# Attention feeding a mixing MLP on one core: the rest keys' P.V moved behind the full keys, the mixing moved half a step, a second operand preparation moved forward

## Chip, cores and metric

One core of a Trainium2 chip runs the whole computation in one program. The metric is device time in microseconds (us), the median of three runs. The engines are PE (matmuls), DVE (vector), ACT (activations), POOL (here only an issuer of DMAs) and SP (issuer of DMAs).

## The reference

Attention with 4 batches, 12 heads, 448 tokens, head size 64, then a token mixing of rank 32 and an MLP of width 3072:

```python
scores = cap * tanh((q @ k.T) / sqrt(D) / cap)
attn = exp(scores - max) / (sum + 1e-9)
x = (attn @ v)                          # heads side by side: [B, S, 768]
u = x + (x.T @ U @ V).T                 # U [448, 32], V [32, 448]
out = u + relu(u @ w_ch1) @ w_ch2       # 768 -> 3072 -> 768
```

## The kernel before

**Order of the work.** The program is written as tasks with priorities, rough durations and buffers (class `Plan`). `simulate` (line 136) plays the tasks through a small model of the five engines and so fixes one order for each engine's queue; `emit` writes the instructions in that order. On the chip every engine works its queue in order and waits at semaphores. A lower priority number goes first. A buffer of a tag is given out strictly in the order in which the tasks were created (`rooms`, line 148): where the next buffer of a tag isn't to be had, later ones of that tag wait too. `SWITCH` (line 88) is what the model charges PE for a change of the task's `mode`.

**Attention.** 24 pairs of heads, worked four pairs at a time (`four`, line 452). The 448 keys of a head are three full tiles of 128 (t = 0, 1, 2) and a rest of 64 keys; the rests of two pairs are put together into one rest tile (t = 3). `steps` lists 14 score tiles for four pairs; two steps share one `th` tile. Each step: scores on PE (L503) into one of two PSUM buffers, tanh on ACT (L510), and per `th` tile one exp in place (L521). For each half (two pairs, h = 0, 1) follow the products with V: the rest keys (`rest`, L546, for both pairs into both banks `o` and `o2`), then the full keys of each pair (`full`, L561), and a copy of each bank to `u` (L274 or L272). For the first half of all, two full tiles run even earlier (`early`, L537). DVE adds up the exp tiles over the key tiles (`es`, L567), which the row sums need.

**Normalizing** (`normalize`, line 585). For two pairs: row sums on PE (L600, with ones) into a `misc` bank, a copy to `sr`, three small DMAs by POOL with a reciprocal between the first two (L607, L616, L611, L624) that bring the reciprocals to all rows as `rb`, and a product on DVE (L629).

**Mixing** (`mixin`, line 634). For two pairs: transposes on PE (L650) into two `misc` banks, copies to `xx`, the U products (L666), a copy to `ys`, the V products (L677, "mix"), and two adds to `u` on DVE (L684). There are two `misc` banks in PSUM for row sums, transposes, U products and mixes. `attention` (line 431) creates the tasks in the order: four pairs, normalize, mix of the two pairs before, normalize, mix and so on; `ys` shares the one slot of `sr`.

**MLP.** Both products run as seven-product (Strassen) multiplications with each fp32 operand split in a high and a low part. The up stage has two passes: batches 0 and 1, then batches 2 and 3, each over twelve chunks (`up_seven`, products L817). `operands` (line 689) prepares seven operand tiles `x` for a pass: terms on DVE (L710), high parts on ACT or DVE (L272, L274), low parts on DVE (L717); its scratch tile `c` is one of the two `wr` buffers into which the weights are loaded too. `strassen_weights` prepares the weights of each chunk in the same way after a conversion (L328, L333, L336) in the first pass. The down stage (L963) runs last; its `g` operands lie in pool `wg`.

The modes of the tasks: scores, transposes and mix "sc", rest scores and rest P.V "q", full P.V "av", row sums and U products "s", all MLP products "mm".

Of the kernel before, what the change touches and what calls it, by code (L numbers as in the profile page):

```python
# [11 lines left out]
F32 = mybir.dt.float32  # L12
F32R = mybir.dt.float32r
# [5 lines left out]
B, H, S, D = 4, 12, 448, 64  # L19
# [18 lines left out]

ALONE = 12
RESTS = 24  # L40
FILL, FIRST = 11, 3
# [45 lines left out]
LAT = {"PE": 240, "ACT": 110, "DVE": 110, "POOL": 150, "SP": 0}  # L87
SWITCH = 210
OVER = {"ACT": 75, "DVE": 60}


class Plan:
# [16 lines left out]
    def task(self, durs, fn, r=(), w=(), prio=0, mode=None, lat=None, begin=0, lock=False, size=0):  # L109


        t = Task()
        t.durs, t.fn, t.prio, t.mode, t.begin, t.lock = durs, fn, prio, mode, begin, lock
        t.lat, t.eng, t.size = lat, None, size
        t.i, t.next, t.at, t.ready = len(self.tasks), [], None, begin
        t.bufs = list(dict.fromkeys([k[0] for k in (*r, *w) if isinstance(k[0], Buf)]))
        for b in t.bufs:
            b.left += 1
        before = set()
        for k in r:  # L120
# [12 lines left out]
        self.tasks.append(t)  # L133
        return t
# [144 lines left out]
class Build(Plan):  # L279
    def __init__(self, tc, qk, v, u, vv, w1, w2, cap, ident, out):  # L280
# [11 lines left out]
        self.pre = Pool("pre", {"th": 7, "qk": 2, "es": 2})  # L292
        self.wg = Pool("wg", {"big": 1, "wb": 2, "g": 3}, after=(self.pre,), shared={"wa": "wb", "ws": "wb"})
        big = F32R, [128, 8 * (DM // 2)]
        self.bx = Pool("bx", {"x": 1}, after=(self.pre,), within=(self.wg, "big"), parts=(*big, {
            "x": [lambda t: t[:, :6 * S].rearrange("p (a d s) -> p a d s", a=2, d=3)]}))
        self.bw = Pool("bw", {"wl": 2}, after=(self.bx,), within=(self.wg, "big"), parts=(*big, {
            "wl": [lambda t, i=i: t[:, 2 * DM * i:2 * DM * i + 2 * DM].rearrange("p (h k s) -> p h k s", h=2, k=2) for i in range(2)]}))
        self.xe = Pool("xe", {"x": 3, "cx": 2}, after=(self.pre,), under=(self.wg,))
        self.an = Pool("an", {"sr": 1, "rb": 1}, side="right", shared={"ys": "sr"})  # L300
        self.aq = Pool("aq", {"r7": 2, "xx": 1, "ust": 1, "vst": 1}, side="right")
# [129 lines left out]
    def attention(self):  # L431
# [8 lines left out]
        for p in range(0, B * NP, 4):  # L440
            self.four(p)
            for q in (p, p + 2):
                self.normalize(q + 1)
                if q:
                    self.mixin((q - 2) // NP, (q - 2) % NP // 2)
        self.mixin(B - 1, NP // 2 - 1)

# [4 lines left out]
    def four(self, p):  # L452
# [32 lines left out]

        steps = [(0, 0), (0, 1), (0, 2), (1, 3), (1, 0), (1, 1), (1, 2), (2, 0), (2, 1), (3, 3), (2, 2), (3, 0), (3, 1), (3, 2)]
        where = {}
# [38 lines left out]
        for h in range(2):  # L526
# [14 lines left out]

            def rest(vn=vn, os=os, rth=rth, rj=rj, ahead=ahead):
                for i in range(2):
                    rows = slice(64 * i, 64 * i + 64)
                    for a in range(2):
                        nc.tensor.matmul(  # L546
                            os[i].t[64 * a:64 * a + 64, :S], vn.t[rows, 6, a], rth.t[rows, rj, a], start=i == 1 or not ahead, stop=False,
                            skip_group_check=ahead and i == 0)

            self.task({"PE": 760}, rest, r=[(vn, 0), (rth, rj)], w=[(o, 0) for o in os], prio=prio, mode="q")  # L550
            for i, o in enumerate(os):
# [5 lines left out]
                def full(i=i, o=o, vn=vn, ts=ts, some=some):  # L557
                    for t in some:
                        th, j = ts[t]
                        for a in range(2):  # L560
                            nc.tensor.matmul(  # L561
                                o.t[64 * a:64 * a + 64, :S], vn.t[:, 3 * i + t, a], th.t[:, j, a], start=False, stop=t == 2)

# [11 lines left out]
                if p < RESTS:  # L575
                    rows = slice(64 * i, 64 * i + 64)
                    some = lambda es=es, rows=rows: es.t[rows]
                    self.task({"DVE": 1090}, partial(add, in0=some, in1=lambda rows=rows, rth=rth, rj=rj: rth.t[rows, rj], out=some),
                        r=[(rth, rj)], w=[(es, 0)], prio=prio, lock=True)
                b, q = divmod(p + i0 + i, NP)  # L580
                u = self.u_bufs[b]
# [3 lines left out]
    def normalize(self, p):  # L585
# [26 lines left out]

        self.task({"PE": 1500 if rest else 750}, sums, r=[(e[0], 0), (e[1], 0), *([(rth, rj)] if rest else [])], w=[(s, 0)], prio=prio, mode="s")
        self.task({"DVE": 620, "ACT": 560}, lambda e: self.copy(e, sr.t, s.t[:, :S]), r=[(s, 0)], w=[(sr, 0)], prio=-300)
# [19 lines left out]
    def mixin(self, b, pp):  # L634
# [33 lines left out]

        self.task({"PE": 450}, products, r=[(xx, 0), (xx, 1), (self.ust, 0)], w=[(yp, 0)], prio=prio, mode="s")
        ys = self.buf("ys", [128, 128], F32, self.an)  # L670
# [18 lines left out]
    def operands(self, bs, order, prio):  # L689
# [4 lines left out]
        xs = {p: self.buf("x", [128, 2, 3, S], F32R, *pools) for p in order}  # L694
        c = self.buf("wr", [128, 3, S], F32, self.wq)
        for p in order:
            for d in range(3):
# [4 lines left out]
                    3: (c, part(0, 1), ALU.subtract, put(c)), 7: (c, part(0, 0), ALU.subtract, part(1, 0))}  # L702
                self.part(p, made, terms, xs[p], put, S, prio, d, lambda t, d=d: (t[:, 0, d], t[:, 1, d]))
        return xs

    def part(self, p, made, terms, t, put, n, prio, d, halves):

# [11 lines left out]
        if p in terms:  # L719
            c, (a, ka), op, (b, kb) = terms[p]  # L720
            made = {p: put(c)}
            self.task({"DVE": 130 + 1.09 * n}, partial(term, out=made[p][0], a=a, op=op, b=b), r=[ka, kb], w=[made[p][1]],
                prio=prio, lock=True)
        src, k = made[p]
        self.task({"ACT": 130 + 0.93 * n, "DVE": 80 + 0.6 * n}, partial(high, src=src), r=[k], w=[(t, 2 * d)], prio=prio)
        self.task({"DVE": 130 + 1.09 * n}, partial(low, src=src), r=[k, (t, 2 * d)], w=[(t, 2 * d + 1)], prio=prio, lock=True)

# [46 lines left out]
    def moe(self):  # L774
# [4 lines left out]
        for n, bs in enumerate(((0, 1), (2, 3))):  # L779
            ws = None if n else self.strassen_weights(0, True, 60000, ALONE - 90, (self.wg,))  # L780
            xs = self.operands(bs, ORDER if n else EARLY, -50 if n else ALONE - 90)
            for c in range(NCH):
                prio = 3 if n or c < NCH - 2 else -60
                ws = ws or self.strassen_weights(c, n == 0, 0, prio)
# [96 lines left out]
    def down_all(self, order, seconds):  # L881
# [29 lines left out]
        for ms in GROUPS:  # L911
            a, b, s2, w, g, bank = {}, {}, {}, {}, {}, {}
            last = ms is GROUPS[-1]
            for x, p in enumerate(PORDER):
# [19 lines left out]
                for n in range(2):  # L934
                    for m in ms:
# [12 lines left out]
                        src = {3: b11, 1: b00, 6: b00, 5: b11, 2: b10, 7: b01, 4: b10}[p]  # L948
                        hi, lo = g[p, n, m] = [self.buf("g", [128, 2, S], F32R, self.wg, *self.gx, self.cr) for _ in range(2)]
                        split(src, (hi, lambda hi=hi: hi.t), (lo, lambda lo=lo: lo.t), size)  # L950
# [95 lines left out]
```

## Time and profile before

| | |
|---|---|
| median of 3 runs | 822.03 us (821.77 to 822.75) |
| the profiled execution, its own time | 822.3 us |
| its span, first to last instruction | 820.5 us |
| mean granted clock of PE | 0.998 |
| busy share of the span | PE 98%, DVE 83%, ACT 58%, POOL 14% |

Attention takes roughly the first 190 us, the up stage goes on to about 509 us, the down stage to about 817 us. The busy share is a mean over these; ACT is far busier in attention than later. A wait in the profile is idle time of an engine just before an instruction, put down to whatever released it.

### The profile page before, as it was taken

How to read it: one execution, taken by the hardware profiler on the slowest of the kernel's cores; microseconds unless marked ns; L12 is line 12 of the kernel's file. 1: busy time of each engine (PE TensorE's matmuls, PEld its weight loads, DVE VectorE, ACT ScalarE, POOL GpSimd, SP SyncE). 2: the span in 40 equal slices, each digit the busy share in tenths (PEclk: the TensorE clock that was granted, in tenths of full speed). 3: DMA queues.
4: the chain of work that ended last, by engine and by line, in shares of the span. 5: the costliest groups of instructions: out<-in, count | busy, mean ns of one | idle time of the engine just before them, and what ended most of it. 6: DMA issues, size and time to landing. Idle time of an engine off the chain costs nothing.

```text
span 820.5 us, 11851 instructions
## 1 busy us (share of the span) xinstructions
PE 803.5 (98%) x4344; PEld 636.9 (78%) x4344; DVE 684.6 (83%) x1083; ACT 473.6 (58%) x670; POOL 111.4 (14%) x182
## 2 busy tenths in 40 slices
PE   9998999999999999999999999999999999999998
PEld 4342333336798999999989998999999999999997
DVE  3778799989989889999787873799999988797763
ACT  7998899995555656666454543436444444433430
POOL 0111111112111111111111111001100011000100
PEclk9999999999999999999999999999999999999999
DMA  6454454444778887548777733975975578524142
GB/s 233 135 162 137 133 155 114 135 142 152 269 261 300 305 294 278 208 156 282 244 237 276 285 134 118 371 233 143 343 255 147 138 241 266 157 69 118 35 135 91
DMA packets 54525, 161.76 MB, mean 197 GB/s; under 512 B 7458, under 2 KB 21314, under 8 KB 54466
## 3 DMA queue, kind: packets, MB, share of 16 engines
q1 hardware_dynamic: 34736, 106.82, 39.6%
q0 software_dynamic: 12816, 35.30, 15.0%
q10 hardware_dynamic: 6914, 18.88, 5.9%
q8 instruction: 34, 0.56, 0.3%
q14 instruction: 25, 0.20, 0.1%
HBM read 106.81 MB, written 46.49 MB: 187 GB/s over the span
## 4 chain that ended last, share of the span: by engine, by line
PE 84%; DVE 8%; DMA 4%; ACT 2%; issue 2%; POOL 0%; ACTq 0%; DVEq 0%; POOLq 0%
PE mm L963 37%; PE mm L817 35%; PE sc L503 4%; PE o L561 3%; DVE es L567 3%; DMA rd<-r 1%; DMA rb<-rd 1%; DMA quad<-wa 1%; PE o L546 1%; DVE x L717 1%; PE misc L424 1%; ACT th L521 1%; ACT th L510 1%; DVE u L629 1%; DVE wr L710 1%
## 5 line engine op out<-in xcount | busy, mean ns | idle before, releaser
L817 PE MATMUL mm<-x,ws 128*128 128x448 f32 x1404 | 289.3, 366 | 3.0 <-ACT cx L272 1.7
L817 PEld LDWEIGHTS mm<-x,ws 128*128 128x128 f32 x1404 | 262.6, 188 | 28.4 <-ACT cx L272 3.9
L963 PE MATMUL mm<-g,bw 128*128 128x448 f32 x756 | 169.4, 366 | 0.0
L963 PE MATMUL mm<-g,wl 128*128 128x448 f32 x756 | 168.0, 365 | 0.0
L963 PEld LDWEIGHTS mm<-g,bw 128*128 128x128 f32 x756 | 142.0, 188 | 11.8
L963 PEld LDWEIGHTS mm<-g,wl 128*128 128x128 f32 x756 | 142.0, 188 | 11.8
L983 DVE TENSOR_TENSOR u<-u,mm 128x448 f32<-128x448 f32 x111 | 67.5, 616 | 42.2 <-PE mm L963 39.2
L272 ACT ACTIVATE g<-gq 128x896 fp32r<-128x896 f32 x62 | 58.1, 946 | 55.6 <-PE mm L963 34.4
L843 POOL DMA_DIRECT2D mid<-cx x96 | 53.3, 555 | 258.6 <-ACT cx L272 250.1
L503 PE MATMUL sc<-qk 64*128 64x448 f32 (+1 forms) x384 | 79.0, 584 | 0.3 <-ACT th L510 0.3
L272 ACT ACTIVATE cx<-mm 128x448 f32<-128x448 f32 x96 | 47.7, 544 | 53.9 <-PE mm L817 49.2
L521 ACT ACTIVATE th<-th,capt 128x1792 f32<-128x1792 f32 x42 | 75.7, 1803 | 0.6
L510 ACT ACTIVATE th<-sc 128x896 f32<-128x896 f32 x80 | 70.4, 929 | 7.9 <-PE sc L503 6.6
L908 DVE TENSOR_TENSOR g<-gq,g 128x896 fp32r<-128x896 f32 x62 | 66.8, 1084 | 3.9 <-ACT g L272 3.7
L272 ACT ACTIVATE st<-mm 128x448 f32<-128x448 f32 x33 | 18.0, 544 | 78.0 <-PE mm L963 44.7
L988 POOL DMA_DIRECT2D u<-st x33 | 28.6, 868 | 249.4 <-ACT st L272 240.6
L567 DVE TENSOR_TENSOR es<-es,th 128x896 f32<-128x896 f32 (+1 forms) x48 | 51.9, 1081 | 12.4 <-ACT th L521 11.9
L272 ACT ACTIVATE cx<-cx 128x448 f32<-128x448 f32 x72 | 41.5, 577 | 34.6 <-DVE cx L830 33.6
L503 PEld LDWEIGHTS sc<-qk 64*128 64x128 f32 (+1 forms) x384 | 27.7, 178 | 41.1 <-issue 16.8
L830 DVE TENSOR_TENSOR cx<-cx,mm 128x448 f32<-128x448 f32 x72 | 44.3, 615 | 17.4 <-PE mm L817 11.2
L561 PE MATMUL o<-th,vn 128*64 128x448 f32 x280 | 58.2, 550 | 0.0
L328 ACT ACTIVATE wa<-wr 128x768 f32<-128x768 f32 (+2 forms) x50 | 44.4, 889 | 18.5 <-DMA quad<-wa 6.5
(98 smaller groups left out, 834.7 us busy)
## 6 DMA issues: line engine op xcount, KB each, us to landing
wr<-in_w SPq DMA_DIRECT2D x48, 768.0 KB, 6.2
mid<-cx POOLq DMA_DIRECT2D x96, 224.0 KB, 4.1
gq<-mid SPq DMA_DIRECT2D x44, 448.0 KB, 6.4
qk<-in_qk SPq DMA_DIRECT2D x23, 448.0 KB, 4.0
kept<-wa ACTq DMA_DIRECT2D x24, 384.0 KB, 6.2
quad<-wa ACTq DMA_DIRECT2D x24, 384.0 KB, 6.5
wb<-quad SPq DMA_DIRECT2D x24, 384.0 KB, 8.2
wa<-kept SPq DMA_DIRECT2D x24, 384.0 KB, 3.6
```

The lines of the kernel that those rows point to most:

```text
L272: e.activation(out=out, in_=in_, func=func)
L328: nc.scalar.activation(out=a_t(), in_=raw_t()[:, 1::2].bitcast(F32), func=AF.Prelu, scale=2.0 ** -112, alpha=-(2.0 ** 32))
L503: nc.tensor.matmul(ps.t[out, a, :S], qks[c].t[hd, 1, 128 * t:min(S, 128 * t + 128)], qks[c].t[hd, 0], start=True, stop=True)
L510: nc.scalar.activation(out=th.t[:, j], in_=ps.t[:, :, :S], func=AF.Tanh, scale=(self.half if t == 3 else self.qsc) if raw else 1.0)
L521: nc.scalar.activation(out=th.t, in_=th.t, func=AF.Exp, scale=self.capt)
L561: nc.tensor.matmul(o.t[64 * a:64 * a + 64, :S], vn.t[:, 3 * i + t, a], th.t[:, j, a], start=False, stop=t == 2)
L567: e.tensor_tensor(out=out(), in0=in0(), in1=in1(), op=ALU.add)
L817: nc.tensor.matmul(ps.t[:, :S], ws[p].t[:, wi, sl], xs[p].t[:, xi, d], start=fresh and n == 0, stop=n == 8, skip_group_check=not fresh)
L843: nc.gpsimd.dma_start(out=self.mid[at][:, c % 2], in_=to(x))
L908: self.task({"DVE": 130 + 1.09 * size}, lambda: nc.vector.tensor_tensor(out=lo(), in0=src.t, in1=hi().bitcast(F32), op=ALU.subtract), r=[( ...
L963: nc.tensor.matmul(ps.t[:, :S], w[p, m].t[:, wi, k, sl], g[p, n, m][gi].t[:, k], start=fresh and i == 0, stop=i == len(at) - 1, skip_group ...
L983: self.task({"DVE": 622}, lambda: nc.vector.tensor_tensor(out=out(), in0=out(), in1=ps.t[:, :S], op=ALU.add), r=[(ps, 0)], w=[key], prio=-200)
```

## The change

- The rest keys' P.V of a half is created after the full keys' P.V of its two pairs, now ends the accumulation in both banks, and reads both banks' keys.
- In `steps` the rest score (1, 3) comes one place later and (3, 3) two places later.
- Each mixing is created one normalize later: the mix of two pairs stands behind the row sums of the two pairs two half steps on. The U products also wait for those sums by a key and get a priority number lower by 20, so go earlier among ready tasks.
- `ys` gets a slot of its own.
- The operands' scratch is no `wr` buffer any more but lies in the room of the later `g` tiles. The operands of the second batches are created before the ninth chunk of the first pass, with ordinary priority, instead of after its last chunk with priority -50; the last two chunks lose their priority of -60.
- `SWITCH` is 150 instead of 210, and nine tasks get their priority nudged.

```diff
+NUDGE = {89: 3, 194: 8, 248: -8, 361: -1, 440: 8, 653: 8, 717: -5, 782: -5, 823: 1}
+NEXT = 8
+LATER = 0
-SWITCH = 210
+SWITCH = 150
+        prio += NUDGE.get(len(self.tasks), 0)
...
-        self.wg = Pool("wg", {"big": 1, "wb": 2, "g": 3}, after=(self.pre,), shared={"wa": "wb", "ws": "wb"})
+        self.wg = Pool("wg", {"big": 1, "wb": 2, "gg": 1}, after=(self.pre,), shared={"wa": "wb", "ws": "wb"})
+        whole = [128, NP, S]
+        self.xc = Pool("xc", {"xc": 1}, after=(self.pre,), within=(self.wg, "gg"), parts=(F32, whole, {"xc": [lambda t: t[:, :3]]}))
+        self.gk = Pool("gk", {"g": 3}, after=(self.xc,), within=(self.wg, "gg"), parts=(F32R, whole, {
+            "g": [lambda t, i=i: t[:, i:i + 2] for i in (0, 2, 4)]}))
-        self.an = Pool("an", {"sr": 1, "rb": 1}, side="right", shared={"ys": "sr"})
+        self.an = Pool("an", {"sr": 1, "rb": 1, "ys": 1}, side="right")
...
                 self.normalize(q + 1)
-                if q:
-                    self.mixin((q - 2) // NP, (q - 2) % NP // 2)
-        self.mixin(B - 1, NP // 2 - 1)
+                if q > 2:
+                    self.mixin((q - 4) // NP, (q - 4) % NP // 2)
+        for q in (B * NP - 4, B * NP - 2):
+            self.mixin(q // NP, q % NP // 2)
...
-        steps = [(0, 0), (0, 1), (0, 2), (1, 3), (1, 0), (1, 1), (1, 2), (2, 0), (2, 1), (3, 3), (2, 2), (3, 0), (3, 1), (3, 2)]
+        steps = [(0, 0), (0, 1), (0, 2), (1, 0), (1, 3), (1, 1), (1, 2), (2, 0), (2, 1), (2, 2), (3, 0), (3, 3), (3, 1), (3, 2)]
...
-            def rest(vn=vn, os=os, rth=rth, rj=rj, ahead=ahead):
...
-                            os[i].t[64 * a:64 * a + 64, :S], vn.t[rows, 6, a], rth.t[rows, rj, a], start=i == 1 or not ahead, stop=False,
-                            skip_group_check=ahead and i == 0)
-            self.task({"PE": 760}, rest, r=[(vn, 0), (rth, rj)], w=[(o, 0) for o in os], prio=prio, mode="q")
...
-                                o.t[64 * a:64 * a + 64, :S], vn.t[:, 3 * i + t, a], th.t[:, j, a], start=False, stop=t == 2)
+                                o.t[64 * a:64 * a + 64, :S], vn.t[:, 3 * i + t, a], th.t[:, j, a], start=t == 0, stop=False)
...
+            def rest(vn=vn, os=os, rth=rth, rj=rj):
...
+                            os[i].t[64 * a:64 * a + 64, :S], vn.t[rows, 6, a], rth.t[rows, rj, a], start=False, stop=True)
+            self.task({"PE": 760}, rest, r=[(vn, 0), (rth, rj), *((o, 0) for o in os)], w=[(o, 0) for o in os], prio=prio, mode="q")
...
-        self.task({"PE": 1500 if rest else 750}, sums, ..., w=[(s, 0)], prio=prio, mode="s")
+        self.task({"PE": 1500 if rest else 750}, sums, ..., w=[(s, 0), ("sums", p)], prio=prio, mode="s")
-        self.task({"PE": 450}, products, r=[(xx, 0), (xx, 1), (self.ust, 0)], w=[(yp, 0)], prio=prio, mode="s")
+        self.task({"PE": 450}, products, r=[(xx, 0), (xx, 1), (self.ust, 0), ("sums", p + 4)], w=[(yp, 0)], prio=prio - (20 if p < 19 else 0), mode="s")
...
-        c = self.buf("wr", [128, 3, S], F32, self.wq)
+        c = self.buf("xc", [128, 3, S], F32, self.xc)
...
-            xs = self.operands(bs, ORDER if n else EARLY, -50 if n else ALONE - 90)
+            xs = more if n else self.operands(bs, EARLY, ALONE - 90)
             for c in range(NCH):
-                prio = 3 if n or c < NCH - 2 else -60
+                prio = 3
+                if not n and c == NEXT:
+                    more = self.operands((2, 3), ORDER, 3)
...
-                        hi, lo = g[p, n, m] = [self.buf("g", [128, 2, S], F32R, self.wg, *self.gx, self.cr) for _ in range(2)]
+                        hi, lo = g[p, n, m] = [self.buf("g", [128, 2, S], F32R, self.gk, *self.gx, self.cr) for _ in range(2)]
```

(`LATER` is the earliest time that the plan gives the second operands; at 0 it does nothing. The early part for the first half of all stays.)

## Rows read from the trace of the kernel before

**Rows 1.** The page's head and its line of busy times, whole span

```profile
span 820.5 us, 11851 instructions
...
PE 803.5 (98%) x4344; PEld 636.9 (78%) x4344; DVE 684.6 (83%) x1083; ACT 473.6 (58%) x670; POOL 111.4 (14%) x182
```

**Rows 2.** Waits of PE, whole span: total us, times, longest us

```profile
PE o L546 <- ACT th L521: 4.4, 4, 1.7
PE mm L817 <- ACT cx L272: 2.3, 4, 0.8
PE misc L677 <- DVE ys L274: 1.8, 1, 1.8
...
PE mm L817 <- DVE cx L830: 1.2, 2, 0.7
PE misc L666 <- DVE xx L274: 0.9, 1, 0.9
PE misc L650 <- DVE u L629: 0.4, 1, 0.4
PE misc L677 <- ACT ys L272: 0.4, 1, 0.4
```

**Rows 3.** Busy time of each engine in two stretches of attention

```profile
20.00:60.00 40.00, 39.87 (x279) 14.51 (x276) 29.97 (x44) 38.26 (x41) 6.27 (x10) 1.00 0.46 137
...
100.00:190.00 90.00, 86.18 (x638) 32.04 (x635) 83.05 (x126) 82.86 (x93) 14.03 (x24) 1.00 0.44 132
```

**Rows 4.** The chain that ended last: start, duration, what

```profile
34.51 1.86 PE sc L503 x12
...
78.17 1.02 PE misc L677 x4
79.19 3.00 PE sc L503 x12
...
90.06 0.45 PE misc L650 x16
...
92.91 0.57 PE misc L666 x16
...
95.19 0.75 PE misc L677 x4
...
187.89 0.95 PE misc L677 x4
```

**Rows 5.** PE in order of time: start, duration, instructions, idle before

```profile
24.42 0.96 PE L600 MATMUL misc<-es,ones 128*32 128x448 f32 x8
...
165.51 0.98 PE L546 MATMUL o<-th,vn 64*64 64x448 f32 x8 [1.69 <-ACT th L521]
...
178.48 0.96 PE L600 MATMUL misc<-es,ones 128*32 128x448 f32 x8
```

**Rows 6.** DVE alone, stretches from 100 to 188 us: length, busy

```profile
100.00:128.80 28.80, 25.63 (x40) 1.00 0.49 150
128.80:142.00 13.20, 13.17 (x25) 1.00 0.44 128
142.00:161.40 19.40, 19.24 (x30) 1.00 0.41 114
161.40:188.00 26.60, 23.04 (x32) 1.00 0.44 138
```

**Rows 7.** DVE instructions on the wr tiles, two of these stretches

```profile
100.00:128.80 28.80, 3.51 (x6) 1.00 0.49 150
...
161.40:188.00 26.60, 3.45 (x5) 1.00 0.44 138
```

**Rows 8.** DVE in order of time, the norm that waited for its DMA

```profile
71.35 1.09 DVE L629 TENSOR_TENSOR u<-u,rb 128x896 f32<-128x896 f32 x1 [1.79 <-DMA rb<-rd]
```

**Rows 9.** Busy time of each engine in two stretches of the up stage

```profile
260.00:300.00 40.00, 40.00 (x199) 36.94 (x198) 35.44 (x70) 23.34 (x41) 6.79 (x12) 1.00 0.87 296
...
340.00:380.00 40.00, 40.00 (x199) 37.01 (x198) 39.15 (x80) 27.53 (x53) 7.18 (x13) 1.00 0.59 191
```

More of the change, by code (lines that the diff above doesn't have):

```diff
@@ L540, in four @@
                 self.task({"PE": 1520}, early, r=[(vn, 0), (th0, 0), (th0, 1)], w=[(os[0], 0)], prio=prio, mode="av")
-            def rest(vn=vn, os=os, rth=rth, rj=rj, ahead=ahead):
[L543 to L546, printed above, removed]
-                            os[i].t[64 * a:64 * a + 64, :S], vn.t[rows, 6, a], rth.t[rows, rj, a], start=i == 1 or not ahead, stop=False,
-                            skip_group_check=ahead and i == 0)
-            self.task({"PE": 760}, rest, r=[(vn, 0), (rth, rj)], w=[(o, 0) for o in os], prio=prio, mode="q")
             for i, o in enumerate(os):
@@ L579, in four @@
                         r=[(rth, rj)], w=[(es, 0)], prio=prio, lock=True)
+            def rest(vn=vn, os=os, rth=rth, rj=rj):
+                for i in range(2):
+                    rows = slice(64 * i, 64 * i + 64)
+                    for a in range(2):
+                        nc.tensor.matmul(
+                            os[i].t[64 * a:64 * a + 64, :S], vn.t[rows, 6, a], rth.t[rows, rj, a], start=False, stop=True)
+            self.task({"PE": 760}, rest, r=[(vn, 0), (rth, rj), *((o, 0) for o in os)], w=[(o, 0) for o in os], prio=prio, mode="q")
+            for i, o in enumerate(os):
                 b, q = divmod(p + i0 + i, NP)
@@ L611, in put @@
             nc.gpsimd.dma_start(out=d.rearrange("a (p f) -> (a p) f", p=32), in_=r7.t)
-        self.task({"PE": 1500 if rest else 750}, sums, r=[(e[0], 0), (e[1], 0), *([(rth, rj)] if rest else [])], w=[(s, 0)], prio=prio, mode="s")
+        self.task({"PE": 1500 if rest else 750}, sums, r=[(e[0], 0), (e[1], 0), *([(rth, rj)] if rest else [])], w=[(s, 0), ("sums", p)], prio=prio, mode="s")
         self.task({"DVE": 620, "ACT": 560}, lambda e: self.copy(e, sr.t, s.t[:, :S]), r=[(s, 0)], w=[(sr, 0)], prio=-300)
@@ L702, in operands, with part @@
                     3: (c, part(0, 1), ALU.subtract, put(c)), 7: (c, part(0, 0), ALU.subtract, part(1, 0))}
-                self.part(p, made, terms, xs[p], put, S, prio, d, lambda t, d=d: (t[:, 0, d], t[:, 1, d]))
+                self.part(p, made, terms, xs[p], put, S, prio, d, lambda t, d=d: (t[:, 0, d], t[:, 1, d]), begin=LATER if bs[0] else 0)
         return xs
-    def part(self, p, made, terms, t, put, n, prio, d, halves):
+    def part(self, p, made, terms, t, put, n, prio, d, halves, begin=0):
         def term(e, out, a, op, b):
@@ L722, in part @@
             self.task({"DVE": 130 + 1.09 * n}, partial(term, out=made[p][0], a=a, op=op, b=b), r=[ka, kb], w=[made[p][1]],
-                prio=prio, lock=True)
+                prio=prio, lock=True, begin=begin)
         src, k = made[p]
-        self.task({"ACT": 130 + 0.93 * n, "DVE": 80 + 0.6 * n}, partial(high, src=src), r=[k], w=[(t, 2 * d)], prio=prio)
-        self.task({"DVE": 130 + 1.09 * n}, partial(low, src=src), r=[k, (t, 2 * d)], w=[(t, 2 * d + 1)], prio=prio, lock=True)
+        self.task({"ACT": 130 + 0.93 * n, "DVE": 80 + 0.6 * n}, partial(high, src=src), r=[k], w=[(t, 2 * d)], prio=prio, begin=begin)
+        self.task({"DVE": 130 + 1.09 * n}, partial(low, src=src), r=[k, (t, 2 * d)], w=[(t, 2 * d + 1)], prio=prio, lock=True, begin=begin)
     def block(self, which, f, first, begin, prio, only=None):
```

## The prediction

> **What bounds the kernel now.** I read the page first, then the waits of PE, then the span cut in stretches, then the chain of waits, and last PE and DVE in order of time. On the page PE is busy 803.5 of 820.5 us [rows 1], so everything that a new order could win on PE lies in 17 us of idle time and in what hides inside the busy time. The waits say where: the rest keys' P.V (L546) waits four times for an exp, 4.4 us in all; the mixing product L677 waits once for a DVE copy, 1.8 us; the U product, the transposes and one more L677 wait 0.9, 0.4 and 0.4 us, all at the start of the up stage; the up products wait 2.3 us for ACT and 1.2 us for DVE [rows 2]. What is left is mostly the first load and the last store, which the change doesn't touch.
>
> In attention PE is not alone. ACT is busy 38.3 of 40 us early on and 82.9 of 90 us from 100 to 190 us [rows 3], so PE and ACT wait for each other in turn: a shorter PE list pays only where ACT isn't itself the end of the chain.
>
> Two costs hide inside busy PE. After the L677 wait the next group of twelve score records took 3.00 us where the same group takes 1.86 [rows 4], and the page's stretches show the granted clock below full there: 1.14 us more. And a change of array mode costs something: L677 takes 0.75 us behind scores, whose mode it shares, and 0.95 behind P.V [rows 4], so 0.20 us a change.
>
> **The change part by part.** No instruction is added or dropped; the same matmuls, copies and DMAs come out in another order, and three small tiles get another home. One half step (two head pairs) lasts 15.4 us: row sums start at 24.42 and, nine sums between them, at 178.48 [rows 5], (178.48 - 24.42) / 10.
>
> Rest keys' P.V last. Today L546 comes first and needs the tile with scores (0,2) and (1,3). The full keys' P.V that now goes first needs (0,2) as well, which stays in that tile, so the same exp still stands in front of it. What helps is other work: the rest products of the pair before (0.9 us) are now free to fall into that hole, and so are older mixing products. Bounds: nothing of the 4.4 us gone, or all; I take two thirds, -2.9 us, since the four waits average 1.1 us (the longest 1.69 [rows 5]) against 0.9 us of rest work. Both P.V banks are now held until the rest products end, so two copies come together; the next P.V is some us behind, and I cost that at nothing while DVE keeps up.
>
> Mode changes. Rest products share a mode with rest scores. Where the order puts them side by side two changes go, 0.4 us, at most twelve times, 4.8 us; nothing asks for it beyond the priorities, the lower SWITCH asks a little less for it, so the other end is 0. I take a quarter, -1.1 us, nearer zero.
>
> Mixing half a step later. Transposes, U product and mix of a pair follow the row sums of two pairs on instead of one. Their norm will long be done, so PE isn't tied to the DMA chain of the reciprocals any more. The 1.84 us wait and the 1.14 us of clock behind it came from a DVE that had stood 1.79 us in the norm of that very pair, waiting for rb [rows 8]. But the norm keeps its place in DVE's queue, and a mix with its copies still passes it. Bounds 0 and -3.0; I take half, -1.5 us. The new wait of the U product on the sums four pairs later costs nothing: the two misc banks are given out in the order of creation, so those sums already stand ahead of the transposes. The extra ys tile removes a wait of ys on sr that no row shows: 0.
>
> What it pushes elsewhere: one mix is 0.45 + 0.57 + 0.75 = 1.77 us of PE [rows 4]. The first leaves the stretch from 20 to 60 us, where ACT is 96% busy [rows 3] and the mix ran for nothing. Between 0 and +1.8 us are paid for it; I take +0.7. At the other end a third mix joins the two that run among the first up products. These two waited 0.9 + 0.4 + 0.4 us [rows 2], 0.85 each. I take +0.5 for the third, with -1.5 and +3 as ends, for its norm is older but DVE is full there.
>
> First batches' operands. They need all mixes of batches 0 and 1, so their start moves by the half step, from 114 to some 129 us. The DVE is full from 128.8 to 161.4 us (13.17 of 13.20, 19.24 of 19.40) [rows 6]. Of this work only what lay before 128.8 us, 3.51 us [rows 7], is new to the time behind; from 142 to 188 DVE has 46.0 - 42.3 = 3.7 us to spare [rows 6]. Besides, the operands' scratch leaves the wr pair, so that the next weights' conversion (3.45 us after 161 us [rows 7]) can go into the hole left at 114 to 129. It fits, narrowly: 0, with +3.5 as the other end, and no gain.
>
> Second batches' operands. They start at the ninth of the twelve chunks (about 300 us) at ordinary priority, where they started near 319 us. PE waits nowhere from 260 to 380 us, with DVE at 35.4 of 40 us before and 39.2 of 40 after [rows 9]. That cover hides them; were it gone, the up products of the second batches would wait on DVE. 0, from -0.5 to +2. The split of the g buffer and the other constants only steer the plan.
>
> **Sum.** -2.9 - 1.1 - 1.5 + 0.7 + 0.5 = -4.3 us. The profiled execution took 822.3 us (span 820.5 and 1.8 around it), so 818.0; it stands 0.27 above the median of the runs, so I predict 817.7 us. 0.2%, about what a measurement of this kernel can tell from no change, is 1.6 us: faster is below 820.4, slower above 823.7.
>
> **Rivals.** (1) ACT bounds attention. For it: ACT's 96 and 92% [rows 3], and that all four L546 waits end with an exp. Then the holes close here and open there, and only the mode changes are won: about 821. Against it: 7 us of ACT idle time from 100 to 190, part of it spent waiting for PE.
>
> (2) The operands come late, the slower one. Place: the DVE between 129 and 188 us. If it doesn't catch up, PE waits 3.5 us for the first up operands, and the next chunk's conversion, 3.45 us [rows 7], slips behind as well: +7.0 on the sum, 825.0, less 0.27: about 824.7. It decides as soon as DVE's backlog at 188 us is over the 4.3 us won before. For it: DVE at 99% [rows 6]; against it: the room freed from 114 to 129.
>
> (3) The norm in the DVE queue. DVE stood 1.79 us for rb with everything behind it late, and PE lost 3.0 us to that [rows 4, 8]. A mix placed half a step later can stand behind the next pair's norm in the same way; two more such events, and nothing won on the first, give -4.3 + 1.5 + 6.0 = +3.2, so 825.2. Against it: one of the ten mixes of attention met it today. The Trainium skill ("TensorE: Matmul & The Clock Gate", the section on the 16 sub-arrays, queue depths) says that VectorE's queue is strictly first in, first out. Here the trace agrees: nothing ran on DVE in those 1.79 us [rows 8]; by that rule alone the delay of the mix frees PE from its own pair's norm and not from the next one's.
>
> (4) More than forecast: all 4.4 and 3.0 us gone, 2.2 of mode changes, +0.5 at the up stage: -9.1, about 813.
>
> **How the numbers follow.** Forecast 0.47, ACT 0.17, late operands 0.18, norm 0.10, more 0.08. The forecast's own range is 814 to 820.4. Faster: 0.45 of the forecast, the 0.08 and a third of ACT, 0.59. Slower: most of the two slow cases, 0.24. The same: 0.17. The range goes from below the 813 of the best case to just above the slow ones, 812 to 825.5; beyond lie the unlikely sums of all bounds on one side.
>
> **What would show it.** Right: the waits of L546 for exps fall from 4.4 to under 2 us and don't come back as waits of L561; no mixing product waits over 1 us in attention, and the clock stays full from 60 to 100 us; the first up product starts some 4 us or more before today's 188.8, less the third mix that now follows. Rest products stand next to rest scores a few times. Wrong: the first up products wait for x or ws; DVE waits for rb at new places with PE behind it; ACT's share in 100 to 190 us stays at 92% and the up stage starts no earlier; or waits appear in 300 to 400 us, where there are none.

## The result and the profile after

The changed kernel took 813.11 us (median of four runs, 811.46 to 814.07) where the kernel before took 821.9 on the same chip: a ratio of 0.9896, 95% interval 0.9879 to 0.9913. The 8.8 us lie inside the predicted range and on the predicted side, but they are twice the 4.3 us of the sum. Medians and spreads here and below are those of a kernel's faster state, which leaves out two of the ten runs with the reciprocal on POOL. The profiled execution took 814.07 us. Its page begins:

```profile
span 812.3 us, 11882 instructions
...
PE 799.8 (98%) x4344; PEld 638.3 (79%) x4344; DVE 679.1 (84%) x1083; ACT 472.8 (58%) x670; POOL 111.2 (14%) x182
```

Beside [rows 1] the span is 8.2 us shorter. PE's busy time fell by 3.7 us for the same 4344 matmuls, its idle time from 17.0 to 12.5 us. So nearly half of the gain lay in what hides inside the busy time.

The waits of PE over the whole span (total us, times, longest us), which answer to [rows 2]; the line numbers have moved, L587 is now the rest P.V, L563 the full P.V, L662, L678 and L689 the parts of the mixing, L831 the up products:

```profile
PE misc L678 <- DVE xx L280: 1.0, 1, 1.0
PE mm L831 <- DVE u L280: 0.9, 1, 0.9
...
PE misc L689 <- ACT ys L278: 0.8, 2, 0.4
PE misc L662 <- DVE sr L280: 0.7, 2, 0.3
...
PE misc L612 <- DVE u L696: 0.5, 1, 0.5
PE o L563 <- ACT th L532: 0.5, 1, 0.5
PE misc L689 <- DVE ys L280: 0.4, 1, 0.4
...
PE mm L831 <- ACT cx L278: 0.3, 1, 0.3
```

The 4.4 us in front of the rest P.V are gone, and 0.5 us came back at L563. The 1.84 us wait of the mixing product is 0.4. The up products' waits for ACT and DVE, 3.5 us before, are 1.2. These three come to 7.6 us less, while PE's idle time fell by 4.5 only: about 3 us came back as small waits elsewhere, such as those of L662 for sr and of L612 for u.

PE in order of time (start, duration, instructions, idle before), joined from two stretches:

```profile
22.44 1.94 PE L514 MATMUL sc<-qk 64*128 64x448 f32 x12
24.20 0.93 PE L587 MATMUL o<-th,vn 64*64 64x448 f32 x8
25.06 0.96 PE L612 MATMUL misc<-es,ones 128*32 128x448 f32 x8
...
63.19 0.98 PE L587 MATMUL o<-th,vn 64*64 64x448 f32 x8
64.11 1.05 PE L612 MATMUL misc<-es,ones 128*32 128x448 f32 x8
65.08 1.94 PE L514 MATMUL sc<-qk 64*64 64x448 f32 x12
66.95 2.48 PE L563 MATMUL o<-th,vn 128*64 128x448 f32 x12
...
72.56 1.02 PE L689 MATMUL misc<-vst,ys 64*128 64x448 f32 x4 [0.41 <-DVE ys L280]
...
181.37 2.12 PE L831 MATMUL mm<-x,ws 128*128 128x448 f32 x9 [0.87 <-DVE u L280]
...
225.91 1.97 PE L831 MATMUL mm<-bx,ws 128*128 128x448 f32 x9
```

At 22.44 the rest scores stand last in their group and the rest P.V follows in the same mode: from one start to the next the scores take 1.76 us and the rest products 0.86. At 65.08 and 63.19 the neighbours have other modes, and the same work takes 1.87 and 0.92. The saving is 0.17 us a join, and 7 of the 12 rest products are joined (none in the kernel before).

The last row is a mark for all that follows: the third group of up products on the tile bx, with the same 162 up products ahead of it in every version's trace. In the kernel before it started at

```profile
231.73 1.99 PE L817 MATMUL mm<-bx,ws 128*128 128x448 f32 x9
```

so 5.8 of the 8.2 us were won up to there, in attention and the start of the up stage, and 2.4 behind it.

The stretches of attention after (length, then busy PE, PEld, DVE, ACT, POOL; granted clock, DMA share, GB/s), for [rows 3], with the stretch between them:

```profile
20.00:60.00 40.00, 39.73 (x256) 14.05 (x256) 29.18 (x43) 39.50 (x41) 6.16 (x10) 1.00 0.52 165
60.00:100.00 40.00, 39.59 (x308) 14.83 (x306) 38.19 (x59) 37.61 (x40) 6.48 (x11) 1.00 0.56 168
100.00:190.00 90.00, 86.85 (x637) 35.61 (x636) 84.71 (x136) 80.28 (x96) 14.80 (x25) 1.00 0.39 120
```

The kernel before had, in the middle stretch,

```profile
60.00:100.00 40.00, 37.24 (x252) 13.23 (x252) 33.12 (x49) 34.14 (x38) 5.75 (x10) 0.96 0.41 138
```

There PE got 56 more matmuls done than before, at a clock of 1.00 instead of 0.96. ACT's share of the third stretch is down from 92 to 89%.

### The profile page after: what moved, and what is told of

It is laid out like the page before. It is cut to its first block, busy times and chain, and to the rows that moved or that the text cites. A ratio compares the mean times of both kernels' runs of the same rounds, so it can differ in the third digit from the quotient of the medians.

```text
span 812.3 us, 11882 instructions
## 1 busy us (share of the span) xinstructions
PE 799.8 (98%) x4344; PEld 638.3 (79%) x4344; DVE 679.1 (84%) x1083; ACT 472.8 (58%) x670; POOL 111.2 (14%) x182
## 4 chain that ended last, share of the span: by engine, by line
PE 81%; DVE 15%; DMA 2%; issue 1%; ACT 0%; POOL 0%; SPq 0%; ACTq 0%; DVEq 0%; POOLq 0%
PE mm L831 36%; PE mm L977 35%; DVE es L569 5%; PE sc L514 4%; PE o L563 2%; DVE x L729 1%; DMA qk<-in_qk 1%; DVE u L696 1%; DVE u L641 1%; DVE wa L346 1%; DVE ws L729 1%; PE misc L434 1%; DVE xc L722 1%; PE misc L612 1%; DVE xx L280 1%
## 5 line engine op out<-in xcount | busy, mean ns | idle before, releaser
L831 PE MATMUL mm<-x,ws 128*128 128x448 f32 x1404 | 288.6, 365 | 1.2 <-DVE u L280 0.9
L831 PEld LDWEIGHTS mm<-x,ws 128*128 128x128 f32 x1404 | 262.9, 188 | 25.3 <-ACT cx L278 1.8
L977 PE MATMUL mm<-g,wl 128*128 128x448 f32 x570 | 148.9, 364 | 0.0
L977 PEld LDWEIGHTS mm<-g,wl 128*128 128x128 f32 x570 | 107.0, 188 | 8.7
L977 PE MATMUL mm<-g,bw 128*128 128x448 f32 x420 | 101.6, 366 | 0.6 <-DVE u L997 0.6
L977 PEld LDWEIGHTS mm<-g,bw 128*128 128x128 f32 x420 | 78.9, 188 | 7.3 <-DVE u L997 0.9
L977 PE MATMUL mm<-gk,bw 128*128 128x448 f32 x336 | 83.0, 367 | 0.0
L977 PEld LDWEIGHTS mm<-gk,bw 128*128 128x128 f32 x336 | 63.1, 188 | 5.4
L844 DVE TENSOR_TENSOR cx<-cx,mm 128x448 f32<-128x448 f32 x72 | 44.4, 617 | 24.8 <-PE mm L831 20.2
L563 PE MATMUL o<-th,vn 128*64 128x448 f32 x280 | 58.1, 548 | 0.5 <-ACT th L532 0.5
L977 PE MATMUL mm<-gk,wl 128*128 128x448 f32 x186 | 56.0, 365 | 0.3 <-DVE gk L922 0.3
```

The lines of the kernel that those rows point to most:

```text
L563: nc.tensor.matmul(o.t[64 * a:64 * a + 64, :S], vn.t[:, 3 * i + t, a], th.t[:, j, a], start=t == 0, stop=False)
L831: nc.tensor.matmul(ps.t[:, :S], ws[p].t[:, wi, sl], xs[p].t[:, xi, d], start=fresh and n == 0, stop=n == 8, skip_group_check=not fresh)
L844: self.task({"DVE": 630}, lambda: nc.vector.tensor_tensor(out=to(x), in0=to(x), in1=bank[onto].t[:, :S], op=ALU.add), r=[key(x), (bank[ont ...
L977: nc.tensor.matmul(ps.t[:, :S], w[p, m].t[:, wi, k, sl], g[p, n, m][gi].t[:, k], start=fresh and i == 0, stop=i == len(at) - 1, skip_group ...
```

## The experiments

All ratios are to the kernel before on the same chip; its median was 820.8 to 822.7 us in the five series. "DVE at DMAs" is the time that DVE stood waiting for a DMA from 20 to 188 us, "mark" the start of the products named above, "behind" the time from the mark to the end of the span, all in us and in the profiled execution.

| version | median us | ratio, 95% | DVE at DMAs | mark | behind |
|---|---|---|---|---|---|
| before | 821.9 | | 3.7 | 231.7 | 588.8 |
| after | 813.1 | 0.9896 (0.9879, 0.9913) | 8.2 | 225.9 | 586.4 |
| after, again | 812.9 | 0.9905 (0.9887, 0.9924) | 4.9 | 222.9 | 586.6 |
| no nudges | 817.3 | 0.9939 (0.9918, 0.9960) | 12.7 | 231.8 | 586.6 |
| no nudges, again | 816.6 | 0.9915 (0.9884, 0.9946) | 6.9 | 227.8 | 586.7 |
| no nudges, rest P.V first | 825.5 | 1.0035 (1.0020, 1.0050) | 7.5 | 232.2 | 590.6 |
| no nudges, mixing early | 821.2 | 0.9998 (0.9983, 1.0012) | 7.4 | 228.2 | 590.7 |
| no nudges, operands as before | 829.6 | 1.0087 (1.0067, 1.0108) | 4.6 | 222.2 | 604.7 |
| after, second operands late | 813.9 | 0.9915 (0.9898, 0.9931) | 8.2 | 225.0 | 588.2 |
| after, SWITCH 210 | 824.9 | 1.0053 (1.0030, 1.0076) | 13.7 | 233.2 | 588.8 |
| before, rest P.V last only | 819.4 | 0.9990 (0.9972, 1.0009) | 7.8 | 231.2 | 589.9 |
| before, SWITCH 150 only | 822.7 | 1.0000 (0.9986, 1.0015) | 1.7 | 232.6 | 588.4 |
| after, reciprocal on POOL | 826.9 | 1.0058 (1.0026, 1.0090) | 16.1 | 236.5 | 588.4 |
| the same, no nudges | 834.8 | 1.0149 (1.0112, 1.0186) | 20.2 | 248.7 | 588.5 |
| after, norms later | 820.9 | 1.0000 (0.9980, 1.0021) | 10.1 | 232.6 | 586.5 |
| the same, no nudges | 822.3 | 1.0006 (0.9980, 1.0032) | 10.6 | 231.2 | 586.7 |
| reciprocal on POOL, norms later | 830.8 | 1.0100 (1.0039, 1.0161) | 15.1 | 241.8 | 588.3 |
| after, first small DMA by SP | 812.9 | 0.9904 (0.9877, 0.9931) | 4.3 | 223.9 | 587.0 |
| after, all small DMAs by SP | 811.9 | 0.9891 (0.9870, 0.9912) | 3.4 | 223.9 | 586.5 |
| first by SP, no nudges | 817.6 | 0.9965 (0.9947, 0.9984) | 6.6 | 226.2 | 589.3 |

### One part undone at a time

The base of this series is the changed kernel without the nudges, since those are numbered by task and would fall on other tasks once a part is undone.

```diff
-NUDGE = {89: 3, 194: 8, 248: -8, 361: -1, 440: 8, 653: 8, 717: -5, 782: -5, 823: 1}
+NUDGE = {}
```

> The changed kernel with an empty NUDGE, as the base of the three next to it. Theory A (the gain comes from the moved parts, the nudges only pick among like orders): 813 to 815 us. Theory B (the nudges close waits of their own): 816 or more, with new PE waits over 1 us in attention.

It took 817.3 us, and 816.6 in a second series:

> The changed kernel with an empty NUDGE once more, as the base of the POOL variant next to it: 816 to 818.5 us.

The waits of PE in that second run:

```profile
PE misc L678 <- DVE xx L280: 3.1, 2, 1.8
PE misc L689 <- DVE ys L280: 1.6, 1, 1.6
```

These two come to 4.7 us where the changed kernel has 1.4, and nothing is lost behind the mark (586.6 and 586.7 us against 586.4). Against the kernel before on the same chip the medians win 4.2 and 6.1 us, where the changed kernel won 8.8 and, repeated below, 7.9. So the nine nudges, which change PE's order in a few places only, are worth some 2 to 5 us, and the prediction gave them nothing. The one pair on a single chip, with the first small DMA by SP (below), says 4.7. The intervals of the first pair, 0.9879 to 0.9913 and 0.9918 to 0.9960, lie apart; that of the repeat reaches into both.

**Rest P.V first again**, on that base:

```diff
-        steps = [(0, 0), (0, 1), (0, 2), (1, 0), (1, 3), ...
+        steps = [(0, 0), (0, 1), (0, 2), (1, 3), (1, 0), ...
...
-            self.task({"PE": 760}, rest, r=[(vn, 0), (rth, rj), *((o, 0) for o in os)], ...
+            self.task({"PE": 760}, rest, r=[(vn, 0), (rth, rj)], ...
```

> As no_nudge, but the rest keys' P.V first again and the old order of the score steps. Theory A: the waits of the rest products for exps come back (about 4 us, against 0.5), so 817 to 818.5. Rival (those waits were filled by the moved mixing, not by the order of the P.V): within 1.5 us of no_nudge, waits under 2 us.

It took 825.45, so 8.2 us more, beyond both expectations. The waits for exps are back only in part (first row, L557 is here the rest P.V); others are larger (second row), and one shows in the order of time what it does to the clock:

```profile
PE o L557 <- ACT th L532: 1.9, 5, 0.6
...
PE misc L611 <- DVE u L695: 2.1, 1, 2.1
...
128.86 3.37 PE L611 MATMUL misc<-es,ones 128*32 128x448 f32 x8 [2.06 <-DVE u L695]
```

Eight row sums that take 0.96 us took 3.37 behind this wait. In the 20 us around it the granted clock averaged 0.91. But only a part of the 8.2 us lies in attention: from the mark to the end this version took 590.6 us, 4 more than its base, though the edit touches nothing there. The planner had found another order for the later stages too.

**Mixing early again**, on the same base:

```diff
-                if q > 2:
-                    self.mixin((q - 4) // NP, (q - 4) % NP // 2)
+                if q:
+                    self.mixin((q - 2) // NP, (q - 2) % NP // 2)
...
-        self.task({"PE": 450}, products, r=[(xx, 0), (xx, 1), (self.ust, 0), ("sums", p + 4)], ..., prio=prio - (20 if p < 19 else 0), mode="s")
+        self.task({"PE": 450}, products, r=[(xx, 0), (xx, 1), (self.ust, 0)], ..., prio=prio, mode="s")
```

> As no_nudge, but each mixing at its old place, ys in the slot of sr, no key and no lower number for the U products. Theory A: the mix's wait for DVE and the fall of the clock behind it come back, some 3 us, so 816 to 817. Rival (the mix costs the same wherever it stands): within 1 us of no_nudge.

It took 821.17, 3.9 us more, above both expectations. PE in order of time shows the wait and the slow clock together:

```profile
106.38 0.64 PE L677 MATMUL misc<-xx,ust 112*32 112x128 f32 x16 [2.31 <-ACT xx L278]
106.95 2.65 PE L513 MATMUL sc<-qk 64*128 64x448 f32 x8
109.38 1.71 PE L688 MATMUL misc<-vst,ys 64*128 64x448 f32 x4
...
116.97 1.77 PE L513 MATMUL sc<-qk 64*128 64x448 f32 x8
```

2.31 us of wait, then 0.88 us more for eight scores (2.65 against 1.77) and 0.8 for a mix (1.71 against 0.92 for an undisturbed one): 4.0 us in one place. Yet the mark, 228.2, is no later than those of the base (231.8 and 227.8), so what was lost here was won elsewhere ahead of the mark. What the version lost lies behind the mark, 590.7 us against 586.6 and 586.7, most of it in waits at the end of the up stage (L830) and the start of the down stage (L976); neither run of the base has these:

```profile
499.94 2.09 PE L830 MATMUL mm<-x,ws 128*128 128x448 f32 x9 [0.68 <-ACT cx L278]
502.74 2.09 PE L830 MATMUL mm<-x,ws 128*128 128x448 f32 x9 [0.71 <-DVE cx L843]
...
507.92 0.47 PE L976 MATMUL mm<-gk,bw 128*128 128x448 f32 x1 [1.86 <-ACT bw L278]
```

So this run doesn't price the place of the mixing by itself; it prices that and another order of everything behind.

**Operands as before**, on the same base: scratch in the wr pair, second operands after the last chunk with the old priorities.

```diff
-        c = self.buf("xc", [128, 3, S], F32, self.xc)
+        c = self.buf("wr", [128, 3, S], F32, self.wq)
...
-            xs = more if n else self.operands(bs, EARLY, ALONE - 90)
+            xs = self.operands(bs, ORDER if n else EARLY, -50 if n else ALONE - 90)
...
-                prio = 3
+                prio = 3 if n or c < NCH - 2 else -60
```

> As no_nudge, but the operands' scratch in a wr buffer again and the second batches' operands after the last chunk with their old priority. Theory A as predicted (operands hidden): within 2 us of no_nudge. Rival (with the mixing later, the scratch holds a wr buffer longer and the next weights come late): 820 or more, with PE waits for ws or x between 180 and 230 us.

It took 829.57, 12.3 us more, and not at the place that was argued: the mark is as early as in the best versions. The loss lies behind 300 us:

```profile
348.62 2.09 PE L825 MATMUL mm<-x,ws 128*128 128x448 f32 x9 [1.08 <-DVE cx L838]
357.98 2.41 PE L825 MATMUL mm<-x,ws 128*128 128x448 f32 x5 [7.27 <-ACT ws L278]
```

### Single parts alone, and the rest of the constants

> The changed kernel once more, as the base of the three next to it: 812 to 814.5 us.

812.88 us: the result repeats.

> The kernel before with only the rest keys' P.V last and the new score steps. Theory A (this part carries most and stands alone): the four waits for exps fall from 4.4 us to under 1, some modes join, so 816.5 to 818.5. Rival (it pays only once the mixing is later): the mix's wait or a DVE wait grows, 820 to 823.

The edit is the two hunks on `steps` and `rest` in the kernel before, with SWITCH 210 and no nudges. Its ratio is 0.9990 (0.9972, 1.0009). The waits for exps are gone, and others stand in their place:

```profile
PE misc L684 <- ACT ys L278: 4.1, 2, 3.0
PE mm L824 <- ACT cx L278: 2.8, 4, 1.2
PE misc L684 <- DVE ys L280: 1.6, 3, 0.6
```

L684 is the mixing product, L824 the up products. The part whose removal cost 8.2 us wins nothing clear of noise by itself.

The second operands alone, undone in the changed kernel by the last two hunks of the diff on operands:

> The changed kernel with the second batches' operands created after the last chunk and with their old priority. As predicted (hidden either way): within 1 us of after_again, the same up to 300 us. Rival (their high priority at the end of the first pass pushes the weights of both passes): 2 to 5 us more, all of it behind 300 us, as PE waits at the end of the up stage or the first down products.

813.91 us, 1.0 more than the changed kernel in the same series (ranges 812.89 to 814.98 and 811.33 to 814.02, so not quite apart). Two waits of 0.7 us each come back at the end of the up stage:

```profile
PE mm L829 <- ACT cx L278: 0.7, 1, 0.7
PE mm L829 <- DVE cx L842: 0.7, 1, 0.7
```

They answer to these two of the kernel before:

```profile
504.35 2.08 PE L817 MATMUL mm<-x,ws 128*128 128x448 f32 x9 [0.68 <-ACT cx L272]
507.14 2.08 PE L817 MATMUL mm<-x,ws 128*128 128x448 f32 x9 [0.71 <-DVE cx L830]
```

In the changed kernel the planner put the first down products between the last up products (from 497.69 us on, where the last up product ends at 502.13), and these waits are gone; here, as in the kernel before, the down products come behind (500.93 and 501.10). The 12.3 us of the version with the operands as before belong to the scratch, or to scratch and late operands together; the scratch alone wasn't tried.

The next run puts one constant back:

```diff
-SWITCH = 150
+SWITCH = 210
```

> The changed kernel with SWITCH 210. As predicted (it only steers): within 1.5 us of after_again. Rival (the order hangs on it): over 3 us more, with the rest products joined to rest scores at other places and PE waits elsewhere.

824.86 us, 12.0 more than the changed kernel on the same chip. It is one constant of the model, and putting it back cost more than undoing any of the named parts but the operands. The nudges stayed in, though, and SWITCH 210 without them wasn't tried, so part of the 12 us may be nudges that don't fit that order. Its longest waits:

```profile
PE mm L831 <- ACT cx L278: 5.6, 5, 3.0
PE misc L612 <- DVE es L569: 2.9, 1, 2.9
PE misc L689 <- DVE ys L280: 2.4, 2, 2.0
```

The same constant in the kernel before, the other way round, with everything else as it was:

> The kernel before with SWITCH 150 and nothing else. Theory A' (the model's price of a mode change decides how readily small tasks are put between others, so it pays alone): 817 to 819. Rival (it pays only with the new order, as the other parts): 820 to 823.

A ratio of 1.0000. A constant that costs 12 us to put back is worth nothing alone.

### Is it DVE standing in front of small DMAs?

In the profiles so far the later marks of the changed order went with more time that DVE stood waiting for DMAs (4.9 us of it with a mark at 222.9, 13.7 with 233.2). The small DMAs of the reciprocals are the most of it. To take the standing in front of the reciprocals off DVE, the reciprocal went to POOL, with the order of the tasks kept. POOL proved so slow at it that the run did the reverse and lengthened the chain:

```diff
-        self.task({"DVE": 250}, lambda: nc.vector.reciprocal(r7.t, r7.t), ...
+        self.task({"DVE": 250}, lambda: nc.gpsimd.tensor_tensor(out=r7.t, in0=r7.t, in1=self.minus, op=ALU.pow), ...
```

> The changed kernel, the order of every queue kept, but the reciprocals of the row sums on POOL (a power of -1) instead of DVE, so that DVE's queue no longer stands at the small DMA before them. Theory C (what is left in attention is DVE standing at DMAs with copies for PE behind it; 2.7 to 4.1 us of such waits in the two profiles): 810 to 812 us, spread between runs smaller. Rival (DVE has other work to wait for anyway): 812.5 to 814. If POOL's power is slow, the norms come late and it is slower.

> The same edit on no_nudge, whose DVE stood 6.3 us at those DMAs. Theory C: 3 to 5 us under no_nudge_again, so the greater part of what the nudges bring. Rival (the nudges win by PE's order alone): within 1.5 us of no_nudge_again.

826.9 and 834.75 us: 13.8 more than the changed kernel (813.1) and 18 more than the one without nudges (816.61), so the theory's gain didn't come. The reciprocal took on POOL (ns, min/median/max)

```profile
L630 POOL TENSOR_TENSOR r<-r,minus x12: 2677/3247/6166, 31.9 to 200.2; 128x14 f32<-128x14 f32 x12
```

against 0.24 us on DVE, and DVE stood in the norm, the last step of the chain, 14.4 us from 20 to 188 us, where the changed kernel had 2.8:

```profile
DVE u L643 <- DMA rb<-rd: 14.4, 6, 4.9
```

The mechanism is therefore real: 3 us more in a side chain that feeds one norm per half step cost some 14 us. The copies behind the norm came late to PE (4.5 us of waits for DVE's ys and 3.1 for its xx from 20 to 230 us, where the changed kernel has 0.4 and 1.0), and the granted clock was 0.96 from 60 to 140 us, where it had been 1.00. Then giving the norm more room should help, so each norm was moved behind the three DVE instructions after it (four with the reciprocal on POOL):

```diff
+        for t in self.norms:
+            i = order.index(t)
+            j, left = i + 1, LATE
+            while left and order[j] not in t.next:
+                left -= order[j].eng == "DVE"
+                j += 1
+            order.insert(j - 1, order.pop(i))
```

> The changed kernel with every norm three DVE instructions later. Theory C: the one wait for rb (2.8 us in one profile, none in the other) is gone: 811 to 812.5, with a smaller spread. Rival: 812.5 to 814.

> no_nudge (816.6 and 817.3 us) with every norm three DVE instructions later. Theory C: DVE's waits at the norm vanish, those at reciprocals stay; 1 to 3 us less, 814 to 816. Rival (es adds and sums now come late behind nothing, PE's order decides): 816 to 818.

> pool_recip (827.4 us, DVE 14.4 us at norms waiting for rb) with every norm four DVE instructions later in the order and nothing else changed. Theory C (time follows DVE's standing at the norm): the waits for rb fall under 5 us and 8 us or more come back, 816 to 819. Rival (POOL's slow power costs in other ways, or PE's order decides): 824 or more.

That simple cure failed: 820.92, 822.28 and 830.84 us, so 8 and 5 us worse than without it, and with the slow reciprocal no better either (4 us more, within overlapping intervals). With DVE's own reciprocal the wait for rb is gone, but the norm now stands behind the next reciprocal, which waits for its own DMA (DVE in order of time, the norm is L642, and the chain's wait total):

```profile
104.94 0.24 DVE L629 RECIPROCAL r<-r 128x14 f32<-128x14 f32 x1 [0.87 <-DMA r<-sr]
105.10 1.03 DVE L642 TENSOR_TENSOR u<-u,rb 128x896 f32<-128x896 f32 x1
106.04 0.28 DVE L281 COPY ys<-misc 128x128 f32<-128x128 f32 x1
...
DVE r L629 <- DMA r<-sr: 8.8, 5, 4.5
```

The remaining way was to shorten the DMAs themselves. In the changed kernel POOL issues them; the one into r carries 7 KB and landed 2.4 to 5.0 us after issue. First this one went to SP, then all three:

```diff
-            nc.gpsimd.dma_start(out=r7.t, in_=sr.t[::32].rearrange("h (p f) -> h p f", p=32))
+            nc.sync.dma_start(out=r7.t, in_=sr.t[::32].rearrange("h (p f) -> h p f", p=32))
...
-            nc.gpsimd.dma_start(out=d.rearrange("a (p f) -> (a p) f", p=32), in_=r7.t)
+            nc.sync.dma_start(out=d.rearrange("a (p f) -> (a p) f", p=32), in_=r7.t)
...
-                nc.gpsimd.dma_start(
+                nc.sync.dma_start(
```

> The changed kernel, every queue's order kept, with the DMA in front of the reciprocals issued by SP instead of POOL (POOL's issue instruction of 0.7 us goes away). Theory C (time follows DVE's standing at DMAs): waits at the reciprocals fall from 2.7 to 4.1 us to under 1.5, 810 to 812 us. Rival (SP, standing at the sums, holds up qk or weight loads queued behind): waits for qk grow, 814 or more.

> As sp_spread, with all the DMAs of the reciprocals (out, back and to all rows) issued by SP. Theory C: waits for rb go too, 809 to 811.5. Rival: SP now stands at the reciprocals as well, three times as often, loads come late: 815 or more.

> The edit of sp_spread with an empty NUDGE (816.6 and 817.3 us without the edit, DVE standing 3.3 and 6.3 us at the reciprocals). Theory C: 813 to 815.5. Rival: no change, 816 to 818.

812.93, 811.87 and 817.64 us, none as low as its theory said. With all three by SP DVE waited 1.3 us for r and nowhere for rb:

```profile
DVE r L628 <- DMA r<-sr: 1.3, 1, 1.3
```

This is the fastest of all versions by its median, but its interval overlaps that of the changed kernel. The second of the three, out of r, now landed 1.4 us after issue all twelve times, where POOL's took 1.7 to 4.2, and the four runs lie within 0.6 us instead of 2.6. Without the nudges the shorter DMA won nothing (817.64 against 816.6 and 817.3): DVE's waits for r fell to 1.0 us there too, but it then stood 5.6 us for loads of q and k, and PE waited

```profile
PE mm L831 <- ACT cx L278: 2.5, 3, 1.6
PE misc L678 <- DVE xx L280: 1.9, 1, 1.9
PE misc L689 <- DVE ys L280: 1.6, 1, 1.6
```

The last two are the waits that the nudges had closed; of the first, 1.6 us lie at 331 us, behind the mark. So what the nudges bring is not the small DMAs alone.

## Why the prediction was right in sign and half in size

**The step that failed** is the last sentence on the parts: "The split of the g buffer and the other constants only steer the plan", taken at 0 without a row. The nine nudges carried some 2 to 5 us: without them PE waited 4.7 us for xx and ys, with them 1.4. Putting SWITCH back, with the nudges left in, cost 12. A smaller miss is the second operands, also at 0, with about 1 us. The sum without the nudges, 817.7, is what the kernel without nudges took, 817.3 and 816.6. But that agreement is partly luck, for the sum had a deeper fault: it added terms as if each stood by itself. Undone one at a time, the rest P.V, the mixing and the operands cost 8.2, 3.9 and 12.3 us, together far more than the 4.2 us that the kernel without nudges had won, and about 4 us of the first and all of the second were lost behind the mark, far from the edit; the rest P.V alone and SWITCH alone won nothing. What one part is worth depends on whether the others have taken away the wait that would come next, and on the order that the planner then finds for all the rest.

Point by point, in the prediction's order, as the changed kernel's trace has it, the nudges' share included:

- **Rest P.V last**, -2.9: as seen from its own waits too small. 4.4 us [rows 2] became 0.5 at L563, so 3.9 gone; how much of it came back among the small new waits isn't shown. In the kernel before, without the later mixing, it did come back, as waits of the mixing product for ys, which the prediction didn't name.
- **Mode changes**, -1.1: right by luck. The term was three joins of twelve at 0.4 us, two changes of 0.20 each; it was seven joins at 0.17, which also gives 1.2.
- **Mixing later**, -1.5: right in kind, too small. The wait went from 1.84 to 0.41 us, and the 1.14 us behind it, priced as the clock, went whole: the stretch from 60 to 100 us ran at 1.00. That is 2.6 of the 3.0 us. The half that was kept back was for the norm in front of the mix; no such event cost PE over 1.0 us.
- **First mix out of the early stretch**, +0.7: no row prices it. PE was as busy from 20 to 60 us (39.73 against 39.87) and ACT went from 38.26 to 39.50, so ACT stood closer to its end there.
- **Third mix in the up stage**, +0.5: about right. Mixing and up products wait 3.4 us from 178 to 230 us, against 3.1 before (0.9, 0.4, 0.4 and 1.4 for cx).
- **First operands**, 0: right. The first up product came at 181.4 instead of 188.8 us, with three mixes behind it and not two.
- **Second operands**, 0, at best -0.5: about -1.0 with the changed kernel's other parts (by the profiles 1.8 behind the mark, 588.2 against 586.4), beyond the end given. The cover named, PE without a wait from 260 to 380 us, held; but the gain lay at 500 us, where the kernel before waited for cx at the stage's end, a place that the prediction had not looked at.

Of the rivals, **ACT bounds attention** fell: ACT's share dropped while the mark came 5.8 us earlier. **Operands late** fell: the first up product came 7.4 us earlier, and the changed kernel's PE has no wait for x or ws. The one big wait for operands and weights, 7.27 us, lay at 358 us and came with the scratch in wr. **The norm in DVE's queue** did not decide this change: DVE stood even longer at DMAs after than before (8.2 against 3.7 us), yet PE lost less. That a mix half a step older has time to spare would explain it; no run shows that by itself. The mechanism is real all the same: with the reciprocal on POOL the kernel took 826.9, over the rival's 825.2, 13.8 us for 11.6 us more of standing at rb, where the rival had put 3.0 us on 1.79. The Trainium skill ("TensorE: Matmul & The Clock Gate", the section on the 16 sub-arrays, queue depths) says that VectorE's queue is strictly first in, first out. The run with later norms agrees: there a norm whose rb was issued from 94.6 us on and landed in 3.3 to 3.7 us stood behind a reciprocal until that one's DMA came, at 104.94. **More than forecast**, 813, is the time that came, with most of the exp waits, most of the mixing's and 1.2 us of mode changes; but it came with the nudges, which that rival didn't count, so the number is partly luck.

**What stays open.** Why one order leaves DVE and ACT waiting less than another: which of the nine nudges closes which of the waits for xx and ys was not taken apart, nor what SWITCH 210 costs without them, nor how far the scratch alone accounts for the 12.3 us. That time at DMAs and mark go together in the changed order is a correlation over a dozen profiles, one execution each; the runs with the slow reciprocal show the cause for that chain, the run with the first DMA by SP and no nudges shows that it isn't the only one. In the kernels with the mixing early or the rest P.V first, before among them (3.7 us, mark at 231.7), it doesn't hold.

## What to carry to other kernels

Where a planner's list fixes every engine's queue, a cost constant or a tie-break is a change like any other: here undoing one cost as much as undoing the largest named part, and it won nothing alone. Don't add up gains of parts that remove waits in the same stretch; ask of each what is late next, and measure it both ways, alone and as the one part undone. Look where in the span the time went before giving it to the edited part: the planner may have changed the order far away. An in-order engine that must wait for a small DMA should do so where what is queued behind it isn't due yet; moving the wait behind the next such wait made it worse here.

## What the runs showed of the hardware that was not expected

- A wait of about 2 us on PE in attention can cost as much again afterwards: 2.06 us were followed by eight matmuls in 3.37 us instead of 0.96, 2.31 us by 0.88 and 0.8 us lost in the next two groups, at a granted clock of 0.91 on the 20 us around. So the level of 1.2 GHz was granted for part of these stretches, after PE had stood. Not every such wait did it: with SWITCH 210 PE waited 2.02 us at 104.68 and 2.86 at 115.96, and the granted clock was 1.00 from 100 to 120 us; the 1.69 us of the kernel before [rows 5] also left it at 1.00 from 160 to 180. After the 1.0 and 0.9 us waits of the changed kernel it stayed full.
- POOL took 2.7 to 6.2 us (median 3.2) for a power over 128x14 values, for which DVE's reciprocal takes 0.24; spans on POOL are rough in this profile.
- The 7 KB DMA out of r landed 1.7 to 4.2 us after issue (median 2.0) with all three small DMAs issued by POOL, and 1.4 us each of the twelve times with all three issued by SP.
- The spread of runs differed between versions: 0.6 us over four runs with all small DMAs by SP, 2.6 over four of the changed kernel, 11.0 over eight with the reciprocal on POOL (822.91 to 833.91). So few runs don't show what sets it.
